# Reordering inside one attention-and-MLP kernel: batch 0's transposes, batch 1's transposes, batch 2's untangling copies and value loads

## The chip, the cores and the metric

The kernel runs on one core of one Trainium2 chip, as one launch. The metric is the device time of a run in microseconds (us). [...] TensorE (PE in the profile) multiplies matrices from SBUF into PSUM, VectorE (DVE), ScalarE (ACT) and GpSimd (POOL) work on elements, and DMAs are issued from the queues of SyncE (SP), ScalarE and GpSimd.

## The reference

Eight batches, eight heads, 576 tokens of 64 dimensions. Attention with a causal mask and a decay (from the cumulated logarithm of a forget gate f), then a two-layer MLP with exact GELU over the 4608 tokens of 512 features:

```python
scores = scale * np.matmul(q, k.transpose(0, 1, 3, 2))
log_f = np.log(np.clip(f, 0.0001, 1.0)); cum = np.cumsum(log_f, axis=-1)
decay = cum[:, :, :, None] - cum[:, :, None, :]
scores = np.where(causal, -1000000000.0, scores + decay)
attn = softmax(scores)                      # over the keys
x = np.matmul(attn, v).transpose(0, 2, 1, 3).reshape(B * S, H * D)
h = x @ w_in                                # 512 -> 2048
out = (0.5 * h * (1.0 + erf(h / sqrt(2)))) @ w_out   # 2048 -> 512
```

## The kernel before

All order is written out by hand: what an engine does next is what the Python text emits next for it.

Heads go in four pairs per batch. A pair needs q and k with the head dimension on partitions (tiles `qkT[0]` to `qkT[3]`, q and k side by side, each used again by the next batch). For batches 0 and 1 TensorE makes them: `transposes_first` (L217) writes q and k of a pair into two PSUM tiles by 64x64 transposes, and VectorE copies each out (L238); `transposes_both` (L240) does q and k in one run of 18 transposes into two PSUM tiles and copies twice (L257). The parameter `near` splits a copy so that the first keys are there early. From batch 2 on, a DMA transpose on SP (`transpose_dma`, L273) fills `tq` and `tk`, and `untangle(b, i)` (L278) brings one pair into token order with eight VectorE copies of 64x288 (L287).

Values are weighed by the decay: `load_v` (L129) fetches them in five pieces by key block into `v_sb`, which has one buffer, and `weigh_v` (L301) multiplies them into `vw` (L306), mostly on GpSimd. `scores` (L317) computes one of four tiles of a pair's scores, ScalarE takes the exponential (L354), and GpSimd clears the part above the diagonal (`affine_select`, L356; pair 0 of batch 1 is masked by TensorE instead). `attend` (L368) multiplies with `vw` into a PSUM tile `o`, and `normalize` (L383) divides (L388, L389) on VectorE. `x_dma` (L413) transposes the result to `xT` by a DMA on SP, from batch 2 on. Batch 0 has its own score tiles: `scores_a`, `scores_b`, `scores_c`, and `scores_t` for the last 64 queries.

PSUM has three pools of two tiles each: `s` for scores, `o` for attention, `m` for MLP sums and transposes. Two `o` buffers serve the two heads of a pair; transposes and sums borrow from the same pools.

`gemm1` (L430) is the first MLP layer with GELU on ScalarE (L450). The second layer of an earlier batch fills TensorE's time during attention: `take(fill, n)` emits n steps of it. In batch 2 that is `gemm2_third`: first `gemm2_second(0)` (L594: sums of row blocks ts 0, in `o`, and ts 1, in `m`, eight steps each, each closed by two VectorE additions, L602 and L554), then PLAN_0 (L534: ts 2 in two `o` banks, ts 3 in two `m` banks, sixteen steps each, each closed by a VectorE copy, L542, and an addition, L554), then PLAN_1 for batch 1. In batch 2 eight steps follow each of the first six score tiles, so pair 0's tiles carry gemm2_second and ts 2, pair 1's first two tiles carry ts 3, and then comes attention of pair 0. In batch 1 `gemm1_hold` keeps some layer-one products of batch 0 in SBUF (L458).

The last stage of the text, the loop over `ffb`, runs the rest of layer one of a batch and, beside it, untangles and weighs for the next batch.

Of the kernel before, what the change touches and what calls it, by code (L numbers as in the profile page):

```python
# [17 lines left out]
D = 64  # L18
# [36 lines left out]
def kernel(  # L55
# [10 lines left out]
    nc = tc.nc  # L66
# [25 lines left out]
    o_psum = ctx.enter_context(tc.tile_pool(name="o_psum", bufs=2, space=PSUM))  # L92
# [589 lines left out]
    def scores_a(i):  # L682
        scores_0([(i, 0, 0, TC)], new_e(0))

    def scores_b(i):
        scores_0([(i, 3, 3 * P, P), (i, 1, P, TC - P)], new_e(2))
# [72 lines left out]
    def first_attention():  # L759

        most = NBLK - 1

        near = (0, 16, D)

        def transposes(i, which, parts=(0, D), pool=m_psum, tag="m"):
            transposes_first(0, i, pool, tag, (which,), parts)

        warm_up(9)
        transposes_first(0, 0, o_psum, "o", (0,))
        transposes_first(0, 0, o_psum, "o", (1,), near, nc.scalar.copy)  # L770
        nc.vector.tensor_tensor_scan(
            decay[:, S - 2 :: -1],
            f_sb[:, S - 1 : 0 : -1],
            none[:, 0 : S - 1],
            2.0**80,
            Alu.mult,
            Alu.add,
        )
        warm_up(2, 2 * P)
        scores_a(0)  # L780
        scores_b(0)
        transposes(1, 0)
        transposes(1, 1, near)
        psw = o_psum.tile([P, NBLK, BH], FP32, tag="o", name="psw")
        for n in range(NBLK):
            nc.tensor.transpose(
                psw[:, n, :], decay[:, K0[n] : K0[n] + P], ident_fp[:BH, :BH]
            )
        scores_a(1)
        nc.vector.tensor_copy(wT[:, 0:4, :], psw[:, 0:4, :])  # L790
        nc.vector.tensor_copy(wT[D:P, 4, :], psw[D:P, 4, :])
        nc.vector.tensor_copy(
            vw(0)[:, :, :, D], wT[:, :, 0:H].rearrange("p n h -> p h n")
        )
        scores_b(1)
        transposes_both(0, 2, m_psum, "m")
        scores_c(0, 1)
        transposes(3, 0, pool=o_psum, tag="o")
        scores_a(2)
        transposes(3, 1, near)  # L800
        scores_b(2)
        weigh_v(0, 0, nc.vector, 0, most)
        weigh_v(0, 1, nc.vector, 0, most)
        load_w_in(0)
        load_v(0, 0, 8, nc.gpsimd, [most])
        load_w_in(1)
        weigh_v(0, 2, n1=most)
        weigh_v(0, 3, n1=most)
        load_w_in(2)
        load_qk_tokens(1, 0, 4)  # L810
        nc.gpsimd.tensor_tensor(
            vw(0)[:, :, most, 0:D],
            v_sb[:, :, most, :],
            wT[:, most, 0:H].unsqueeze(2).to_broadcast([P, H, D]),
            Alu.mult,
        )
        nc.gpsimd.memset(v_sb[:, :, 0, 0:1], 0.0)
        load_v(1, 0, 4, nc.gpsimd)
        load_w_in(3)
        load_qk_tokens(1, 4, 8)  # L820
        load_v(1, 4, 8, nc.gpsimd)
        scores_a(3)
        first_tail = scores_t(0, True)
        scores_c(2, 3)
        attend_0(0, 0)
        attend_0(0, 1)
        scores_b(3)
        attend_0(1, 0)
        attend_0(1, 1)
        first_tail()  # L830
        attend_0(2, 0)
        to_xT_0(0, nc.scalar.copy)
        second_tail = scores_t(2)
        attend_0(2, 1)
        to_xT_0(1, nc.scalar.copy)
        attend_0(3, 0)
        to_xT_0(2, nc.scalar.copy)
        second_tail()
        scores_t4()
        attend_0(3, 1)  # L840

        pss = [gemm1(0, 0, (0, 1)), gemm1(0, 1, (0, 1), spare())]
        for ffb in range(2):
            gemm1(0, ffb, (2,), pss[ffb])
        pss.append(gemm1(0, 2, (0, 1, 2), spare()))
        to_xT_0(3, nc.vector.tensor_copy)
        fourth = s_psum.tile([P, 2, 512], FP32, tag="s", name="ps1")
        pss.append(gemm1(0, 3, (0, 1, 2), fourth[:, 0, :]))
        for ffb in range(4):
            gemm1(0, ffb, (HP - 1,), pss[ffb])  # L850
# [23 lines left out]
    def attention(b):  # L874


        fill = gemm2_third() if b == 2 else gemm2_rows(b - 1, PLAN)
        counts = FILL_2 if b == 2 else FILL

        def av(i, n=0):  # L880
            for h in range(2):
                attend(b, i, h, (0, 1, 2, 3, 4))
                normalize(b, i, h)
                if h == 0:
                    take(fill, n)
            x_dma(b, i)

        for i in range(HP):
            for t in range(4):
                scores(b, i, t)  # L890
                take(fill, counts[i][t])
                if t == 1 and 0 < i < (HP if b == 2 else HP - 1):
                    av(i - 1)
                    if b == 2 and i == 1:
                        load_v(3)
                if b == 2 and (i, t) == (0, 3):
                    weigh_v(b, 2)
                    weigh_v(b, 3)
                if b > 2 and i == 0 and t == 1:
                    load_v(b + 1)  # L900
                if b > 2 and t == 0 and i < 2:
                    transpose_dma(b + 1, 4 * i, 4 * i + 4)
                if b == 2 and t == 1 and i == 1:
                    transpose_dma(3, 0, 4)
        if b == 2:
            take(fill, 4)
            av(HP - 1)
        else:
            av(HP - 2)
            take(fill, 3)  # L910
            av(HP - 1, 1)
            put_off.pop()()
        take(fill, 4)
        if b == 2:
            transpose_dma(3, 4, 8)
        take(fill, 999)

        pss = [gemm1(b, ffb, (0, 1)) for ffb in range(2)]
        for ffb in range(2):
            gemm1(b, ffb, (2,), pss[ffb])  # L920
        pss += [gemm1(b, ffb, (0, 1, 2), spare()) for ffb in (2, 3)]
        for ffb in range(4):
            gemm1(b, ffb, (3,), pss[ffb])
        more = s_psum.tile([P, 2, 512], FP32, tag="s", name="ps1")
        gemm1(b, 4, ps=more[:, 0, :])
        if b + 1 < B:
            untangle(b + 1, 0)
            weigh_v(b + 1, 0)
        x_tail(b)

    def second_attention():


        b, fill = 1, gemm2_first(0)

        def av(i, h):
            attend(b, i, h, (0, 1, 2, 3, 4))
            normalize(b, i, h)

        def transposes(i, pool, tag):  # L940
            transposes_first(b, i, pool, tag)


        nc.scalar.activation(warm[0:1, 0:1], warm[0:1, 0:1], Act.Exp)
        def tiles(i, t):
            scores(b, i, t)
            scores(b, i, t + 1)

        def run(i):
            av(i, 0)  # L950
            av(i, 1)

        tiles(0, 0)
        transposes(1, o_psum, "o")
        gemm1_hold(10)
        gemm1_hold(11)
        tiles(0, 2)
        gemm1_hold(12, nc.scalar.copy)
        transposes(2, o_psum, "o")
        tiles(1, 0)  # L960
        gemm1_hold(13)
        run(0)
        tiles(1, 2)
        gemm1_hold(14, nc.scalar.copy)
        transposes(3, o_psum, "o")
        weigh_v(1, 2)
        tiles(2, 0)
        gemm1_hold(15)
        run(1)
        weigh_v(1, 3)  # L970
        tiles(2, 2)
        take(fill, 4)
        tiles(3, 0)
        transpose_dma(2, 0, 4)
        transpose_dma(2, 4, 8)
        to_xT(b, 0, nc.vector.tensor_copy, o_psum, "o")
        to_xT(b, 1, nc.vector.tensor_copy, o_psum, "o")
        take(fill, 4)
        tiles(3, 2)
        behind(qk_of[2][1], H - 1)  # L980
        load_w_out(2)
        load_w_out(3)
        run(2)
        take(fill, 4)
        av(3, 0)
        take(fill, 4)
        both = s_psum.tile([P, 2, 1024], BF16, tag="s", name="ps_x2")
        to_xT(b, 2, nc.scalar.copy, ps=both[:, 0, 0:XC])
        av(3, 1)
        gemm1_begin(1, both)  # L990
        x_tail(1)
        load_v(2)

    for b in range(B):
# [6 lines left out]
        for ffb in range(4 if b < 2 else 5, n_ff):  # L1001
# [20 lines left out]
            elif b + 1 < B:  # L1022
                first, gap = (5, 3) if b == 1 else (1, 4)
                at, late = divmod(ffb - first, gap)
                if late == 0:
                    untangle(b + 1, at)
                if late == gap - 2 and (b > 1 or at < 2):
                    weigh_v(b + 1, at)
                if ffb == (9 if b == 1 else 14):
                    load_qk_tokens(b + 2)  # L1030
# [34 lines left out]
```

## Time and profile before

| what | us |
|---|---|
| median of 3 runs (lowest, highest) | 335.41 (334.63, 336.61) |
| the profiled execution | 335.99 |
| its span, first to last instruction | 334.2 |
| TensorE busy | 324.5 |
| ScalarE, VectorE, GpSimd busy | 206.0, 184.0, 134.2 |
| untangling copies (L287), 192 of them | 82.7 busy |
| weighing products on GpSimd (L306), 30 | 38.3 busy |
| batch 1's attention begins, batch 2's begins (first scores on TensorE) | 33.1, 67.0 |
| batch 2's first layer begins, batch 3's attention begins | 99.2, 113.8 |

Times within the execution count from the first instruction of the span. A row of the timeline names the start, the length, the engine, the source line and the operation, and merges neighbours of one kind; "x4" is four of them. In brackets stands the idle time of the engine before the row, and what ended it. In the list of waits the three numbers are the total, the number of waits and the longest one. A line of SPq or POOL with DMA in its operation is the issue of a transfer, not the transfer.

### The profile page before, as it was taken

Reading aid. Unit: us, or ns where it says so; the run is one execution under the profiler, and the core shown is the slowest. Engines: PE = TensorE matmul, PEld = TensorE weight load, DVE = VectorE, ACT = ScalarE, POOL = GpSimd, SP = SyncE. Lnnn points to the kernel's source line nnn. Section 1 sums busy time; section 2 is a strip of 40 time slices with the busy share of each in tenths; the row PEclk is TensorE's granted clock in tenths of the full one; section 3 lists DMA queues with packets and bytes.
Section 4 is the critical chain, followed back from the end, with each engine's and each line's share of the span. In section 5 each row is a group of like instructions: output and inputs, shape, how many; then the busy total and the mean of one; then the engine's idle time right before and its main releaser. Section 6 shows DMA issues by size and latency. Waiting matters only on the chain.

```text
span 334.2 us, 7948 instructions
## 1 busy us (share of the span) xinstructions
PE 324.5 (97%) x3233; PEld 169.2 (51%) x3233; DVE 184.0 (55%) x426; ACT 206.0 (62%) x298; POOL 134.2 (40%) x260
## 2 busy tenths in 40 slices
PE   8799999999999999999999999999999999999995
PEld 4554555445544466445644565455544654444443
DVE  5852755674549755894589547954796450010011
ACT  4876886964525786478736891798278846405600
POOL 8985973038327054704471354434532420000000
PEclk9999999999999999999999999999999999999998
DMA  8899999979999999489939896879600320021022
GB/s 125 193 198 220 189 185 138 180 160 160 204 179 184 152 207 156 99 131 196 190 107 140 167 204 122 125 144 186 178 2 1 103 73 31 2 88 38 2 50 77
DMA packets 94948, 44.18 MB, mean 132 GB/s; under 512 B 74176, under 2 KB 89792, under 8 KB 94912
## 3 DMA queue, kind: packets, MB, share of 16 engines
q1 hardware_dynamic: 77760, 27.16, 40.8%
q0 software_dynamic: 16752, 15.99, 30.3%
q8 instruction: 25, 0.41, 0.5%
q10 hardware_dynamic: 400, 0.52, 0.4%
q14 instruction: 11, 0.09, 0.1%
HBM read 36.85 MB, written 9.44 MB: 139 GB/s over the span
## 4 chain that ended last, share of the span: by engine, by line
PE 74%; DMA 13%; POOL 8%; DVE 3%; issue 1%; SPq 1%; POOLq 0%
PE ps L430 29%; PE ps L534 25%; PE ps L474 8%; PE o L375 7%; PE s L325 5%; DMA k<-in_k_dram 4%; DMA tq<-q 3%; DMA q<-in_k_dram 3%; DMA xT<-x 2%; POOL v_sb L169 2%; DVE qkT L287 2%; POOL v_sb L134 1%; POOL vw L306 1%; POOL q L120 1%; POOL k L120 1%
## 5 line engine op out<-in xcount | busy, mean ns | idle before, releaser
L450 ACT ACTIVATE g<-ps 128x512 bf16<-128x512 f32 x138 | 78.4, 602 | 80.7 <-PE ps L430 80.2
L430 PE MATMUL ps<-xT,w_in_sb 128*128 128x512 bf16 x512 | 114.1, 379 | 0.9 <-DMA xT<-x 0.6
L534 PE MATMUL ps<-w_out_sb,g 64*128 64x512 bf16 (+1 forms) x711 | 108.5, 377 | 0.3 <-DVE ot L554 0.3
L354 ACT ACTIVATE e<-s 128x896 bf16<-128x896 f32 x112 | 87.7, 836 | 21.5 <-PE s L325 16.4
L430 PEld LDWEIGHTS <-w_in_sb 128*128 128x128 bf16 x576 | 55.3, 98 | 68.1 <-issue 3.6
L356 POOL TENSOR_SCALAR_AFFINE_SELECT e<-e 128x256 bf16<-128x256 bf16 (+1 forms) x135 | 49.1, 384 | 88.3 <-ACT e L354 87.9
L534 PEld LDWEIGHTS <-g 64*128 64x128 bf16 (+1 forms) x711 | 40.3, 95 | 34.9 <-issue 4.8
L306 POOL TENSOR_TENSOR vw<-v_sb,wT 128x640 bf16<-128x640 f32 (+1 forms) x30 | 38.3, 1280 | 26.7 <-DMA v_sb<-in_v_dram 16.8
L287 DVE COPY qkT<-tk 64x288 bf16<-64x288 bf16 x96 | 42.0, 437 | 4.0 <-DMA tk<-k 2.4
L287 DVE COPY qkT<-tq 64x288 bf16<-64x288 bf16 x96 | 40.7, 424 | 3.6 <-DMA tq<-q 2.2
L542 DVE COPY ot<-ps 128x512 f32<-128x512 f32 x20 | 13.8, 692 | 48.1 <-PE ps L534 48.1
L325 PE MATMUL s<-qkT 64*128 64x256 bf16 (+2 forms) x336 | 37.5, 276 | 0.8 <-DVE qkT L238 0.6
L375 PEld LDWEIGHTS <-e 128*128 128x128 bf16 x840 | 30.3, 98 | 7.9 <-POOL e L356 2.5
L483 DVE COPY ot<-ps 128x512 f32<-128x512 f32 (+2 forms) x9 | 5.7, 632 | 49.6 <-PE ps L474 49.6
L375 PE MATMUL o<-vw,e 128*128 128x65 bf16 x840 | 32.3, 194 | 0.0
L389 DVE TENSOR_TENSOR x<-o,r 128x320 bf16<-128x320 f32 x56 | 27.5, 492 | 1.9
L474 PE MATMUL ps<-w_out_sb,g 128*128 128x512 bf16 (+2 forms) x144 | 28.0, 355 | 0.0
L325 PEld LDWEIGHTS <-qkT 64*128 64x128 bf16 x336 | 16.9, 94 | 19.1 <-issue 4.2
L474 PEld LDWEIGHTS <-g 128*128 128x128 bf16 x144 | 13.5, 98 | 14.5
L554 DVE TENSOR_TENSOR ot<-ot,ps 128x512 f32<-128x512 f32 x22 | 15.1, 685 | 1.1
L388 DVE RECIPROCAL r<-o 128x5 f32<-128x5 f32 x56 | 10.5, 188 | 9.1 <-PE o L375 9.1
L430 PE MATMUL ps<-tails,w_in_sb 128*128 128x512 bf16 x64 | 14.3, 377 | 0.0
(88 smaller groups left out, 181.9 us busy)
## 6 DMA issues: line engine op xcount, KB each, us to landing
out_dram<-ot SPq DMA_DIRECT2D x32, 256.0 KB, 2.3
v_sb<-in_v_dram SPq DMA_DIRECT2D x24, 256.0 KB, 5.0
q<-in_q_dram POOLq DMA_DIRECT2D x6, 576.0 KB, 6.6
k<-in_k_dram POOLq DMA_DIRECT2D x6, 576.0 KB, 8.7
v_sb<-in_v_dram POOLq DMA_DIRECT2D x17, 128.0 KB, 5.6
w_in_sb<-in_moe_w_in_dram POOLq DMA_DIRECT2D x4, 512.0 KB, 8.1
w_out_sb<-in_moe_w_out_dram POOLq DMA_DIRECT2D x4, 512.0 KB, 8.3
v_sb<-in_v_dram SPq DMA_DIRECT2D x6, 128.0 KB, 4.5
```

The lines of the kernel that those rows point to most:

```text
L287: nc.vector.tensor_copy(rows[:, odd], src[odd * D : (odd + 1) * D, 2 * i + h].rearrange("d j p -> d p j"),)
L306: eng.tensor_tensor(vw(b)[:, hs, n0:n1, 0:D], v_sb[:, hs, n0:n1, :], w.unsqueeze(3).to_broadcast([P, 2, n1 - n0, D]), Alu.mult,)
L325: nc.tensor.matmul(st[:, h, c + z : c + w], kT[i][d, K0[n] : K0[n] + P], qT[i][d, q0 + z : q0 + w], start=c == 0 or not on_pe, stop=not on_pe,
L354: nc.scalar.activation(et[:, :, z:c], st[:, :, z:c], Act.Exp, scale=scale)
L356: nc.gpsimd.affine_select(out=et[:, :, c0 + z : c0 + P], in_=et[:, :, c0 + z : c0 + P], compare_op=Alu.is_ge, fill=0.0, base=z, pattern=[[ ...
L375: nc.tensor.matmul(o[:, m, :], e_of[b, i, t][:, h, c : c + P], vw_of[b][:, 2 * i + h, n, :], start=(n == 0), stop=(n == m),)
L389: nc.vector.tensor_tensor(x_of[b, i][:, :, h, :], o[:, :, 0:D], r.unsqueeze(2).to_broadcast([P, NBLK, D]), Alu.mult,)
L430: nc.tensor.matmul(ps, w_in_sb[:, kt, ffb * P : (ffb + 1) * P], src[:, kt, 0:TC], start=(kt == 0), stop=(kt == n_dm - 1),)
L450: nc.scalar.activation(g_of[c][ffb], ps, Act.Gelu)
L474: nc.tensor.matmul(pss[ts][:, c0:c1], g_of[c][kt][:, ts * P : (ts + 1) * P], w_out_sb[:, kt, c0:c1], start=(kt == 0), stop=(kt == n_ff - 1),)
L534: nc.tensor.matmul(banks[r], g_of[c][kt][rows, ts * P : (ts + 1) * P], w_out_sb[rows, kt, :], start=kt == (steps.index("r") if r else 0), ...
L554: nc.vector.tensor_tensor(ot, ot, bank, Alu.add)
```

## The change

Batch 0: q of pair 1 is transposed between the first two score tiles. Pair 2's q and k are transposed one by one around `scores_b(1)`, with the copies of the decay weights in between, and pair 3's in one run (before: pair 2's in one run, pair 3's one by one). The first attention matmuls come ahead of the tail scores. Batch 1: pair 2's transposes come behind attention of pair 0. Batch 2: pairs 2 and 3 are untangled in the attention stage, after the steps of the second and the third score tile, not in the loop of layer one of batch 1; the values of batch 3 are loaded by GpSimd in three portions, not by SP in one.

```diff
@@ first_attention @@
-        def transposes(i, which, parts=(0, D), pool=m_psum, tag="m"):
-            transposes_first(0, i, pool, tag, (which,), parts)
+        def transposes(i, which, parts=(0, D)):
+            transposes_first(0, i, m_psum, "m", (which,), parts)
...
         scores_a(0)
+        transposes(1, 0)
         scores_b(0)
-        transposes(1, 0)
         transposes(1, 1, near)
...
         scores_a(1)
+        transposes(2, 0)
+        scores_b(1)
         nc.vector.tensor_copy(wT[:, 0:4, :], psw[:, 0:4, :])
+        transposes(2, 1, near)
         nc.vector.tensor_copy(wT[D:P, 4, :], psw[D:P, 4, :])
...
-        scores_b(1)
-        transposes_both(0, 2, m_psum, "m")
         scores_c(0, 1)
-        transposes(3, 0, pool=o_psum, tag="o")
         scores_a(2)
-        transposes(3, 1, near)
+        transposes_both(0, 3, m_psum, "m")
         scores_b(2)
...
         scores_a(3)
-        first_tail = scores_t(0, True)
         scores_c(2, 3)
         attend_0(0, 0)
+        first_tail = scores_t(0, True)
         attend_0(0, 1)
@@ attention(b) @@
                 if t == 1 and 0 < i < (HP if b == 2 else HP - 1):
                     av(i - 1)
-                    if b == 2 and i == 1:
-                        load_v(3)
+                if b == 2 and i == 0 and t in (1, 2):
+                    untangle(b, t + 1)
+                if b == 2 and i > 1 and t == 0:
+                    load_v(3, eng=nc.gpsimd, ns=(2 * i - 4, 2 * i - 3))
...
         if b == 2:
+            load_v(3, eng=nc.gpsimd, ns=(4,))
             transpose_dma(3, 4, 8)
@@ second_attention @@
         gemm1_hold(12, nc.scalar.copy)
-        transposes(2, o_psum, "o")
         tiles(1, 0)
         gemm1_hold(13)
         run(0)
+        transposes(2, o_psum, "o")
         tiles(1, 2)
@@ the loop over ffb @@
-                if late == 0:
+                if late == 0 and (b > 1 or at < 2):
                     untangle(b + 1, at)
```

## The prediction

> **What bounds the kernel now.** I read the page first, then TensorE's waits, then the order of VectorE and GpSimd around the start of batch 2, which most of the change moves.
>
> ```profile
> PE 324.5 (97%) x3233; PEld 169.2 (51%) x3233; DVE 184.0 (55%) x426; ACT 206.0 (62%) x298; POOL 134.2 (40%) x260
> ```
>
> TensorE is busy for 324.5 of 334.2 us, so an edit gains only what it takes out of the 9.7 us of gaps and loses whatever gap it opens. Its waits by name, longest in total first:
>
> ```profile
> PE ps L430 <- DMA xT<-x: 0.6, 2, 0.4
> ...
> PE ps L534 <- DVE ot L554: 0.3, 1, 0.3
> ```
>
> Both can be won here. The second comes at 71 us: PLAN_0's matmuls (L534) wait for the sum that empties their PSUM bank. The timeline of VectorE shows why the sum is late (start, length, then who):
>
> ```profile
> 68.90 1.34 DVE L287 COPY qkT<-tk 64x288 bf16<-64x288 bf16 x4
> 70.28 0.69 DVE L602 TENSOR_TENSOR ot<-ot,ps 128x512 f32<-128x512 f32 x1
> 71.00 0.69 DVE L554 TENSOR_TENSOR ot<-ot,ps 128x512 f32<-128x512 f32 x1
> 71.61 0.68 DVE L602 TENSOR_TENSOR ot<-ot,ps 128x512 f32<-128x512 f32 x1
> 72.32 0.69 DVE L554 TENSOR_TENSOR ot<-ot,ps 128x512 f32<-128x512 f32 x1
> 75.52 0.69 DVE L542 COPY ot<-ps 128x512 f32<-128x512 f32 x1 [2.52 <-PE ps L534]
> ```
>
> The first sums stand behind the last untangling copies (L287), 16 of which run from 64.83 to 70.25, 0.34 apart. GpSimd is idle until 71.99, then runs without a gap:
>
> ```profile
> 71.99 1.28 POOL L306 TENSOR_TENSOR vw<-v_sb,wT 128x640 bf16<-128x640 f32 x1 [16.77 <-DMA v_sb<-in_v_dram]
> ...
> 73.38 1.27 POOL L306 TENSOR_TENSOR vw<-v_sb,wT 128x640 bf16<-128x640 f32 x1
> ...
> 74.73 0.84 POOL L120 DMA_DIRECT2D q<-in_q_dram  x1
> 75.56 0.78 POOL L120 DMA_DIRECT2D k<-in_k_dram  x1
> 76.34 1.72 POOL L356 TENSOR_SCALAR_AFFINE_SELECT e<-e 128x256 bf16<-128x256 bf16 x5
> 78.03 1.27 POOL L306 TENSOR_TENSOR vw<-v_sb,wT 128x640 bf16<-128x640 f32 x1
> ```
>
> **Batch 0.** No instruction is added: pair 3 takes the joint transposes (18, then copies of 1.78 us) that pair 2 had, and pair 2 the two single sets. In order, with these rows: pair 1's q copy can start at 7.55 (end of the scan) instead of 7.83, so scores_a(1) goes at 8.60 (before 8.87); scores_a(2) needs only single copies and goes near 11.1 (before 12.55, its largest stall, 1.0). But scores_a(3) now needs the joint copies: the last tokens land at 11.56, transposes to 12.3, copies to 14.1, scores at 14.17 (before 14.14). ScalarE has lost 0.25 us less by then and scores_b(3) goes at 16.03 (before 16.28). The copies that weigh pair 0 and 1 follow at 14.1 as at 14.2 before. I take -0.25, between 0 (scores_a(3) alone) and -0.5 (if the tail scores, now behind the first attention matmuls, free PSUM sooner).
>
> **Batch 1.** Pair 2's transposes (0.41 us) go behind run(0). They need both buffers of the o pool, which run(0) has just filled; before, 1.3 us of scores and held gemm1 lay between run(0) and the next transposes. New order: run(0) near 38.85 (39.31, less 0.25 from batch 0, less the 0.41 of the transposes, plus 0.2 for a score buffer that ScalarE frees at 37.74), VectorE's held copy to 39.73, two reciprocals and products end at 41.05 (before 41.45), transposes end 41.5, next scores 41.5 against 40.35: +1.15 with batch 0's gain in it. Bounds: 0 (buffers free in time) to +1.4 (pair 3's transposes then wait for pair 2's copies of 1.42).
>
> **Batch 2, the untangling.** 16 copies move from 64.83 to behind the second pair of sums, and PLAN_0's bank emptying (L542 at 75.52, L554 at 76.25) stands behind all 16. Those banks are the o buffers in which attention of pair 0 accumulates, so TensorE, which started it at 79.24, waits for them. Gained: the stall at 71.03, 0.6 us from one L534 matmul to the next beyond its 0.11. The copies no longer have GpSimd idle, and that is their price:
>
> ```profile
> 102.21 1.27 DVE L287 COPY qkT<-tk 64x288 bf16<-64x288 bf16 x1
> ```
> ```profile
> 101.96 1.34 POOL L306 TENSOR_TENSOR vw<-v_sb,wT 128x640 bf16<-128x640 f32 x1
> ```
> ```profile
> 139.69 1.35 DVE L287 COPY qkT<-tk 64x288 bf16<-64x288 bf16 x1
> ```
>
> The same copy takes 1.27 instead of 0.33: begun inside a GpSimd product, it ends at 103.48, 0.18 after that product's end at 103.30. The one at 139.69 ends at 141.04, 0.16 after the DMA issue on GpSimd at 140.11 (0.77) ends. So a copy begun under a GpSimd instruction ends 0.17 after it. For the selects no row has an overlap; the nearest is GpSimd's plain copy at 54.80 (0.42), where the untangling copy also ended 0.18 after it. I let them hold; without it 0.5 us less.
>
> With batches 0 and 1 TensorE is 1.2 late: its matmuls for the second sums end at 72.2 (71.00 before), two sums of 0.72 end at 73.65, and attention would be due at 79.24 + 1.2 - 0.6 = 79.84. Copy by copy: ends 74.82 (second product), 75.17 free, 76.50 (issues), 76.95, 77.30, 77.89, 78.24 (selects), 79.48 (third product); pair 3: 80.86 (fourth product, 79.42 to 80.68), 81.36, 81.72, 82.05 (pair 1's selects), four free to 83.4. Then L542 and L554, 0.72 apart, to 84.9, the same for ts 3 to 86.3. Attention starts near 84.2, and PLAN_1's second matmul, which needs the last bank, at 86.35 against 80.60: +5.75. Batches 0 and 1 are inside that number: had TensorE come 1.2 earlier, the sum would still be near +5.5, because GpSimd's start at 71.99 is set by the landing of v. Ends: +5.0 (selects do not hold) and +6.
>
> [...]
>
> **Batch 2, v of batch 3.** SP loses this:
>
> ```profile
> 83.21 7.25 SPq L134 DMA_DIRECT2D v_sb<-in_v_dram  x5
> ```
>
> Behind it stood tokens' transposes, a store, and pair 1's xT, ready at 86.95 and issued at 94.80; pairs 2 and 3 went at 97.66, and gemm1 stalled at 100.63. Now the transposes come at 83.2 (k's waits for tokens that land at 86.21; stores and xT behind it lose nothing), and xT is in time: -0.6. GpSimd gets five issues of 0.75. Two fall at about 84.6, two at 90, where it is busy 2.45 us of 6; the fifth after the last select, so weighing pair 0 (95.17 before) waits for a landing near 99 to 101, with tails, further weighing and batch 4's tokens behind it. Attention needs it at 120.04, so the cover is some 18 us; its loss would be the difference alone. I take 0.
>
> **Clock.** By the working above TensorE would stand idle from about 79.9 (attention due at 79.84) to 84.2, then works in bursts until 86.35. Windows at the end of the kernel (length, busy times by engine, granted clock third from the right):
>
> ```profile
> 330.00:332.00 2.00, 0.11 (x2) 0.00 (x0) 0.29 (x1) 0.00 (x0) 0.00 (x0) 1.00 0.48 122
> 332.00:334.20 2.20, 0.00 (x0) 0.00 (x0) 0.00 (x0) 0.00 (x0) 0.00 (x0) 0.60 0.05 12
> ```
>
> The last matmul ends near 330.1, and a mean of 0.60 means half speed from about 332.4, 2.3 us later. At the start nine warm-up matmuls come 0.42 apart instead of 0.216: 1.9 us lost. Ends: 0 and 1.9; part of a slow stretch would fall on attention that waits anyway, so +1.5.
>
> [...]
>
> **Sum.** The profiled execution took 335.99 (span 334.2 and 1.8 around it), 0.6 above the median of 335.41. +5.75 - 0.6 + 1.5 = +6.65: 342.6 against the profiled one, 342.0 against the median.
>
> **Rivals.** *The clock holds* (or the selects don't): +5.0 or +5.75, less 0.6: 339.8 to 340.6. For it: attention's bursts; against: 2.3 us sufficed at the end. 25%.
> *Copies run free of GpSimd*: 16 at 0.34 from 73.65 end at 79.1, four bank emptyings at 81.95 against 80.60, +1.35 - 0.6: 336.2. Against it, every copy that began inside a product was stretched. 7%.
> *Not slower: GpSimd waits instead of VectorE, and batch 1's buffers are free in time.* The second sums end at 72.2, copies at 77.65, emptyings at 80.5, no later than before: -0.1 - 0.6: 334.7. It decides if a copy takes under 0.36 us beside GpSimd. 7%.
> *Half speed lasts two such stretches*: +8.5 or more, 344. 8%.
>
> **How the numbers follow.** Forecast 53%. A measurement of this kernel tells 0.5%, 1.7 us, from no change. Slower by more: forecast, holding clock and double stretch, 0.86. Same: 336.2 and half of 334.7, 0.10; the other half, should the first of these gains be larger than sized, 0.04, is faster. The range from 338.8 (+5.0 less 0.6, less 1 for other errors) to 344.0 leaves out the two free-copy cases and the tail above.
>
> **What would show it.** Right: L287 copies of 0.5 to 1.4 us between 72 and 84, L542 of ts 2 near 83.5, a TensorE wait of over 3 us on it before attention (L375) of batch 2, v_sb gone from SP, gemm1's stall at its start gone, and 1 us between run(0) and transposes in batch 1. Wrong: L287 copies all near 0.33 after 72 us, or attention of batch 2 starting before 81.

## The result and the profile after

The change makes the kernel slower: 343.84 us against 335.45, medians of six runs each (342.99 to 345.41; before 334.63 to 337.60), ratio 1.0247 with a 95% interval of 1.0206 to 1.0288. The profiled execution took 343.30 (span 341.2), before 335.99 (334.2). The prediction, 342.0 in a range of 338.8 to 344.0, had the sign and the main mechanism; it was 1.8 too low, and three of the six executions took more than 344.0. Two executions of the experiments below are left out of their ratios as slow ones: the profiled one of b3 (420.06 us at a mean clock of 0.755) and one of a1 (341.69, 0.985).

The page's line of engines and, below it, TensorE's waits (total, count, longest), both of after:

```profile
PE 322.2 (94%) x3191; PEld 169.9 (50%) x3233; DVE 189.0 (55%) x426; ACT 206.4 (60%) x298; POOL 139.1 (41%) x265
```
```profile
PE o L375 <- DVE ot L542: 4.9, 1, 4.9
PE s L637 <- DVE qkT L257: 1.4, 1, 1.4
...
PE ps L430 <- DMA xT<-x: 0.4, 1, 0.4
```

The first wait is new: attention's matmuls (L375) wait for the copy that empties their PSUM bank (L542). The second is in batch 0 (see b2), the third in the first layer of batch 5 (212.34). VectorE is 5 us busier with the same 426 instructions, so some of them take longer. Both are in the timelines of after, TensorE first (start, length, who; in brackets the wait):

```profile
78.08 1.46 PE L534 MATMUL ps<-w_out_sb,g 64*128 64x512 bf16 x12
79.69 0.38 PE L534 MATMUL ps<-w_out_sb,g 128*128 128x512 bf16 x1 [0.16 <-issue]
84.93 1.81 PE L375 MATMUL o<-vw,e 128*128 128x65 bf16 x30 [4.86 <-DVE ot L542]
```

VectorE in the same stretch:

```profile
73.14 0.69 DVE L554 TENSOR_TENSOR ot<-ot,ps 128x512 f32<-128x512 f32 x1
73.75 2.18 DVE L287 COPY qkT<-tq 64x288 bf16<-64x288 bf16 x4
75.94 5.52 DVE L287 COPY qkT<-tk 64x288 bf16<-64x288 bf16 x4
81.48 1.33 DVE L287 COPY qkT<-tq 64x288 bf16<-64x288 bf16 x4
82.82 1.33 DVE L287 COPY qkT<-tk 64x288 bf16<-64x288 bf16 x4
84.19 0.69 DVE L542 COPY ot<-ps 128x512 f32<-128x512 f32 x1
...
85.52 0.69 DVE L542 COPY ot<-ps 128x512 f32<-128x512 f32 x1
86.31 0.69 DVE L554 TENSOR_TENSOR ot<-ot,ps 128x512 f32<-128x512 f32 x1
```

VectorE is never idle here. Sixteen copies stand between the second sums (L554 at 73.14) and L542, which ran at 75.52 before. Eight of them take 0.33 each; four take 5.52 together. The next timeline, GpSimd's in after, shows beside what:

```profile
72.73 1.27 POOL L306 TENSOR_TENSOR vw<-v_sb,wT 128x640 bf16<-128x640 f32 x1
...
74.17 0.84 POOL L120 DMA_DIRECT2D q<-in_q_dram  x1
75.00 0.78 POOL L120 DMA_DIRECT2D k<-in_k_dram  x1
75.78 1.82 POOL L356 TENSOR_SCALAR_AFFINE_SELECT e<-e 128x256 bf16<-128x256 bf16 x5
77.57 1.27 POOL L306 TENSOR_TENSOR vw<-v_sb,wT 128x640 bf16<-128x640 f32 x1
...
78.96 1.27 POOL L306 TENSOR_TENSOR vw<-v_sb,wT 128x640 bf16<-128x640 f32 x1
80.18 0.22 POOL L313 CAST vw<-wT 128x10 bf16<-128x10 f32 x1
80.33 1.28 POOL L356 TENSOR_SCALAR_AFFINE_SELECT e<-e 128x256 bf16<-128x256 bf16 x3
```

The products (L306) keep their 1.27, as when VectorE is idle (1.27 at 73.38 in before), and the copies pay. The clock, as windows cut at its edges (length, busy times by engine, granted clock third from the right):

```profile
80.07:82.40 2.33, 0.00 (x1) 0.00 (x0) 2.26 (x6) 0.00 (x0) 1.54 (x5) 1.00 1.30 203
82.40:84.82 2.42, 0.00 (x0) 0.00 (x0) 2.32 (x7) 0.00 (x0) 0.00 (x0) 1.00 0.12 18
84.82:88.23 3.41, 3.30 (x38) 2.21 (x39) 3.20 (x8) 0.90 (x1) 0.00 (x0) 0.50 0.31 118
```

TensorE stands still from 80.07 at full clock; when it resumes, the clock is at half for 3.41 us. Four of the six executions have a mean clock of 0.990 (spans 341.4 to 343.3), two, the profiled one among them, 0.995 (340.8, 341.2): half speed for 3.41 us of 341 lowers the mean by 0.005, so four of the six have lost as much as two such stretches; only the profiled execution shows where its stretch lay.

By stages on TensorE (start times in the span, before to after): the first layer-one run loses a wait of 0.27 us, so that its third matmul comes at 21.85 instead of 22.18 (-0.33; b6, which does not have batch 0's edit, lacks that wait too), batch 2's first scores 67.02 to 68.39 (so batch 1 costs +1.70), batch 2's attention 79.24 to 84.93, its layer one 99.18 to 106.32, batch 3's first scores 113.75 to 120.31, end 334.2 to 341.2. SP issues no load of v in this batch any more, and layer one runs without the stall that it had at 100.63 (99.18 to 113.75 is 14.57 us before; 13.99 in after).

### The profile page after: what moved, and what is told of

Its sections match the earlier page's. It is cut to its first block, busy times and chain, and to the rows that moved or that the text cites. A ratio compares the mean times of both kernels' runs of the same rounds, so it can differ in the third digit from the quotient of the medians.

```text
span 341.2 us, 7909 instructions
## 1 busy us (share of the span) xinstructions
PE 322.2 (94%) x3191; PEld 169.9 (50%) x3233; DVE 189.0 (55%) x426; ACT 206.4 (60%) x298; POOL 139.1 (41%) x265
## 4 chain that ended last, share of the span: by engine, by line
PE 88%; DVE 6%; ACT 2%; issue 2%; DMA 1%; ACTq 0%
PE ps L430 35%; PE ps L534 23%; PE ps L474 8%; PE o L375 8%; PE s L325 6%; DVE qkT L287 3%; DMA xT<-x 1%; PE ps_w L210 1%; PE ps L594 1%; PE ps_f L228 1%; PE s L637 1%; ACT e L354 1%; PE o L703 1%; PE ps L570 1%; ACT e L673 1%
## 5 line engine op out<-in xcount | busy, mean ns | idle before, releaser
L430 PE MATMUL ps<-xT,w_in_sb 128*128 128x512 bf16 x494 | 112.5, 379 | 1.6 <-DMA xT<-x 0.4
L534 PE MATMUL ps<-w_out_sb,g 64*128 64x512 bf16 (+1 forms) x692 | 105.0, 378 | 1.6 <-issue 1.3
L534 PEld LDWEIGHTS <-g 64*128 64x128 bf16 (+1 forms) x711 | 39.6, 95 | 35.1 <-issue 5.0
L306 POOL TENSOR_TENSOR vw<-v_sb,wT 128x640 bf16<-128x640 f32 (+1 forms) x30 | 38.3, 1281 | 27.6 <-DMA v_sb<-in_v_dram 19.3
L287 DVE COPY qkT<-tk 64x288 bf16<-64x288 bf16 x96 | 46.0, 480 | 1.6
L287 DVE COPY qkT<-tq 64x288 bf16<-64x288 bf16 x96 | 41.9, 437 | 1.4
L375 PE MATMUL o<-vw,e 128*128 128x65 bf16 x840 | 33.0, 195 | 5.7 <-DVE ot L542 4.9
L325 PE MATMUL s<-qkT 64*128 64x256 bf16 (+1 forms) x336 | 37.4, 277 | 0.9 <-DVE qkT L238 0.6
L542 DVE COPY ot<-ps 128x512 f32<-128x512 f32 x20 | 13.8, 692 | 43.6 <-PE ps L534 43.5
L375 PEld LDWEIGHTS <-e 128*128 128x128 bf16 x840 | 31.0, 99 | 12.9 <-issue 6.8
L554 DVE TENSOR_TENSOR ot<-ot,ps 128x512 f32<-128x512 f32 x22 | 15.1, 685 | 1.1
```

Of the source, the lines that this page charges most:

```text
L287: nc.vector.tensor_copy(rows[:, odd], src[odd * D : (odd + 1) * D, 2 * i + h].rearrange("d j p -> d p j"),)
L306: eng.tensor_tensor(vw(b)[:, hs, n0:n1, 0:D], v_sb[:, hs, n0:n1, :], w.unsqueeze(3).to_broadcast([P, 2, n1 - n0, D]), Alu.mult,)
L325: nc.tensor.matmul(st[:, h, c + z : c + w], kT[i][d, K0[n] : K0[n] + P], qT[i][d, q0 + z : q0 + w], start=c == 0 or not on_pe, stop=not on_pe,
L375: nc.tensor.matmul(o[:, m, :], e_of[b, i, t][:, h, c : c + P], vw_of[b][:, 2 * i + h, n, :], start=(n == 0), stop=(n == m),)
L430: nc.tensor.matmul(ps, w_in_sb[:, kt, ffb * P : (ffb + 1) * P], src[:, kt, 0:TC], start=(kt == 0), stop=(kt == n_dm - 1),)
L534: nc.tensor.matmul(banks[r], g_of[c][kt][rows, ts * P : (ts + 1) * P], w_out_sb[rows, kt, :], start=kt == (steps.index("r") if r else 0), ...
```

## The experiments

The theory after the result: the untangling copies, slowed by GpSimd's products and standing before the bank emptyings, make TensorE wait; the wait costs clock on top; batch 1's order costs about 1 us, which is partly hidden in that wait; batch 0 and the loads are worth little. Each kernel is compared with before on the same chip (its medians there: 335.49 for a1 to a4, 335.14 for b1 to b4, 334.99 for b5, b6, c3 and e1). A difference from after is taken between medians of different chips, so some tenths of it can be the chip.

**a1: the change without its untangling.**

```diff
-                if b == 2 and i == 0 and t in (1, 2):
-                    untangle(b, t + 1)
...
-                if late == 0 and (b > 1 or at < 2):
+                if late == 0:
                     untangle(b + 1, at)
```

> The changed kernel with pairs 2 and 3 of batch 2 untangled in batch 1's layer-one loop again. Theory (the copies stand before the bank emptying, GpSimd holds them, attention waits, the clock falls): the 4.9 us wait and the half-speed stretch go, and the rest of the change stays: batch 0 -0.3, batch 1 +1.2, loads -0.6, so 335.7 (335 to 336.5), within 0.3% of the kernel before. Rival (the values' loads on GpSimd or batch 1 carry part of the loss): above 338.

Measured 337.07, ratio 1.0060 (1.0026 to 1.0094). VectorE and TensorE of a1:

```profile
76.48 0.69 DVE L542 COPY ot<-ps 128x512 f32<-128x512 f32 x1 [2.37 <-PE ps L534]
```
```profile
80.19 1.11 PE L375 MATMUL o<-vw,e 128*128 128x65 bf16 x30
```

VectorE now waits for TensorE, not the reverse, and attention starts without a wait. This one edit costs 6.8 us (343.84 less 337.07). What is left is 1.6 above before, more than the 335 to 336.5 expected.

**a2: before with the untangling moved, and nothing else** (a1's lines the other way round).

> The kernel before with only the untangling of pairs 2 and 3 moved. Theory: GpSimd's start near 72 sets the end of the copies, so nearly the whole loss shows without the other edits: +6 to +9, 341.5 to 344.5, and a wait of attention of batch 2 of 4.5 to 6 us. Rival (the loss needs TensorE late by batch 1's edit): under +4.

Measured 343.51, ratio 1.0239 (1.0201 to 1.0277): 8.0 us. VectorE, then TensorE, of a2:

```profile
72.89 3.49 DVE L287 COPY qkT<-tq 64x288 bf16<-64x288 bf16 x4
76.40 6.04 DVE L287 COPY qkT<-tk 64x288 bf16<-64x288 bf16 x4
82.45 1.54 DVE L287 COPY qkT<-tq 64x288 bf16<-64x288 bf16 x4
84.01 1.34 DVE L287 COPY qkT<-tk 64x288 bf16<-64x288 bf16 x4
```
```profile
86.12 1.81 PE L375 MATMUL o<-vw,e 128*128 128x65 bf16 x30 [6.90 <-DVE ot L542]
```

TensorE is at its bank earlier than in after, and the copies end later: GpSimd's first product begins at 73.12, when v has landed, against 71.34. So the end of the wait is set by GpSimd, not by TensorE: in after, a2, a4 and b4 the copy that is held longest ends 9.2 to 9.3 us after that first product begins, whenever TensorE arrives. Alone this edit costs 8.0, on top of the other three 6.8: their costs do not add. Here the clock was at half for two stretches (6.83 us from 83.73).

**a3: after, with the two products of pairs 2 and 3 later.**

```diff
-                if b == 2 and (i, t) == (0, 3):
+                if b == 2 and (i, t) == (1, 2):
                     weigh_v(b, 2)
                     weigh_v(b, 3)
```

> The changed kernel with GpSimd's weighing of pairs 2 and 3 of batch 2 moved from behind pair 0's fourth score tile to behind pair 1's third, so that two of GpSimd's four products no longer stand beside the copies. Theory (a copy waits for the GpSimd instruction under way): the copy of 3.6 us at 77 becomes one of 0.3 to 0.5, VectorE is done 2.5 to 3 us earlier, TensorE's wait falls from 4.9 to near 2 us and half speed mostly goes: 338 to 340. Rival (16 copies in front are the loss, GpSimd has no part): no change, 343.8.

Measured 340.81, ratio 1.0165 (1.0109 to 1.0220): 3.0 less than after, though 0.8 above the range expected. VectorE, GpSimd and TensorE of a3:

```profile
73.99 2.87 DVE L287 COPY qkT<-tq 64x288 bf16<-64x288 bf16 x4
76.87 2.37 DVE L287 COPY qkT<-tk 64x288 bf16<-64x288 bf16 x4
```
```profile
76.70 3.12 POOL L356 TENSOR_SCALAR_AFFINE_SELECT e<-e 128x256 bf16<-128x256 bf16 x8
...
86.29 1.28 POOL L306 TENSOR_TENSOR vw<-v_sb,wT 128x640 bf16<-128x640 f32 x1
```
```profile
82.82 1.52 PE L375 MATMUL o<-vw,e 128*128 128x65 bf16 x30 [2.51 <-DVE ot L542]
```

With two products gone from beside the copies, the second four take 2.37 instead of 5.52 and the wait falls from 4.86 to 2.51. That the copies are slowed by GpSimd is thereby shown: VectorE's own list is the same. Beside the selects alone the four still take 0.59 each on average instead of 0.33 (one 1.04, three 0.43).

**a4: after, with TensorE kept busy in the wait** by 22 matmuls that nothing reads.

```diff
+                if b == 2 and (i, t) == (1, 1):
+                    both = s_psum.tile([P, 2, 512], FP32, tag="s", name="ps_w")
+                    for _ in range(22):
+                        nc.tensor.matmul(
+                            both[:, 0, :], warm[:, 0:P], warm, start=True, stop=True
+                        )
```

> The changed kernel with 22 added matmuls of 128x512 on zeros (some 4.75 us) in TensorE's wait ahead of attention of pair 0 of batch 2, into a score buffer; their result is used by nothing. Theory (the wait lets the clock fall to half for 3.4 us or more): the wait itself stays, attention's 30 matmuls take 0.9 us instead of 1.6, no half-speed stretch, -1.7 to -3.4: 340.5 to 342. Rival (attention is slow there because of what VectorE and GpSimd do): 343.8 or more.

Measured 342.56 (342.30 to 342.87), ratio 1.0209 (1.0166 to 1.0252): 1.3 less than after, 0.6 above the range expected, and the spread shrinks from 2.4 us to 0.6. TensorE of a4:

```profile
79.91 4.91 PE L895 MATMUL ps_w<-warm 128*128 128x512 bf16 x22
84.83 1.35 PE L375 MATMUL o<-vw,e 128*128 128x65 bf16 x30
...
86.95 1.02 PE L534 MATMUL ps<-w_out_sb,g 64*128 64x512 bf16 x7 [0.25 <-DVE ot L554]
```

Attention starts when it did in after, at full clock, and ends 0.6 earlier. It still takes 1.35 instead of 1.11, not the 0.9 expected, which fits its second o bank being emptied only at 85.50 (L554). Then TensorE stands before the next bank, which also was late. So the clock's price is 1.3 by the medians; in the profiled execution with its one stretch 0.58 (attention to layer one 21.39 in after, 20.81 here, 19.95 in a1). The other 0.86 to a1 is late banks, the second of ts 2 and those of ts 3.

**b1: before with batch 1's edit alone.**

```diff
-        transposes(2, o_psum, "o")
         tiles(1, 0)
         gemm1_hold(13)
         run(0)
+        transposes(2, o_psum, "o")
```

> The kernel before with only batch 1's edit (pair 2's transposes behind attention of pair 0). Theory (both o buffers are still full): TensorE waits 1.1 to 1.3 us in front of these transposes and nothing gives it back: span +1.0 to +1.3, 336.5. Rival (the wait is given back by later waits, the sums at 71 us above all): +0.6, as the stall of 0.6 there falls away for a TensorE that comes 1.2 later, 336.1 or less.

Measured 336.23, ratio 1.0039 (1.0024 to 1.0055): +1.1. TensorE of b1:

```profile
39.14 1.11 PE L375 MATMUL o<-vw,e 128*128 128x65 bf16 x30
40.81 0.22 PE L228 MATMUL ps_f<-key_of,k 64*64 64x64 bf16 x2 [0.55 <-DVE r L388]
41.44 0.47 PE L228 MATMUL ps_f<-key_of,k 64*64 64x64 bf16 x34 [0.41 <-DVE x L389]
41.84 0.50 PE L325 MATMUL s<-qkT 64*128 64x448 bf16 x4
```

The transposes need the two o tiles that attention has just filled, and wait for both divisions. The next scores start at 41.84; before they started at 40.35, with attention only 0.17 later (39.31), so the place costs 1.66 us in the traces. By the medians it is 1.1; whether other executions of before lose 0.6 us somewhere that b1 does not is open.

**b4: after with batch 1's edit taken back.**

> The changed kernel with batch 1's edit undone. Theory (the end of the copies in batch 2 hangs on GpSimd's start, set by the landing of v, not on TensorE): TensorE comes 1.2 us earlier and waits as much longer, total -0.6 to +0.5 against the changed kernel, 343.2 to 344.3, the wait before attention 5.5 to 7 us. Rival (the costs add): -1.2, 342.6, the wait still 4.9.

Measured 343.50, ratio 1.0253 (1.0231 to 1.0275): 8.4 us above before on its chip, just as after is on its own, not 1.2 less. In its profiled execution TensorE came to batch 2 no earlier (68.63) and waited 5.15, less than the 5.5 to 7 expected, because its clock was at half from 15.01 to 18.42 in batch 0; without such a fall the comparison would be cleaner. The hiding is seen better in a1 and a2.

**b2: before with batch 0's edit alone.**

> The kernel before with only batch 0's edit. Theory: TensorE starts the first layer 0.3 us earlier, span -0.3, 335.1. Rival (the one long wait of 1.5 us for the joint copies that replaces several shorter ones leaves TensorE so little work in one stretch that the clock falls in some executions): median near 335.3, but some executions 3 to 6 us longer at a granted clock under 0.99.

Measured 335.30, ratio 1.0022 (0.9994 to 1.0050): no gain. TensorE of b2:

```profile
11.64 0.39 PE L637 MATMUL s<-qkT 64*128 64x512 bf16 x2 [0.25 <-ACT e L673]
14.67 0.39 PE L637 MATMUL s<-qkT 64*128 64x512 bf16 x2 [1.38 <-DVE qkT L257]
```

The stall of 0.98 that stood at 12.55 before is gone from pair 2 and is back at pair 3 as 1.38: the joint copies are late for whichever pair gets them. Runs above 338 us come in all three kernels in which this edit stands without the untangling (a1 three of ten, up to 341.69; b2 two of twelve; b5 below), in a1 and b2 with a mean clock of 0.977 to 0.988; before did not exceed 337.6, nor did b1, b6, c3 or the eleven other runs of b3. The clock can fall in batch 0 without this edit too: in c3's trace it is at half from 14.17 to 17.58, in a run of 335.08.

**b5: b2 with six matmuls that nothing reads ahead of scores_a(3)**, to see if that wait is where the clock is lost.

```diff
+        idle = o_psum.tile([P, TC], FP32, tag="o", name="ps_w")
+        for _ in range(6):
+            nc.tensor.matmul(idle, warm[:, 0:P], warm, start=True, stop=True)
         scores_a(3)
```

> The kernel before with batch 0's edit and six added matmuls of 128x512 on zeros in the 1.4 us wait ahead of scores_a(3), whose result nothing uses. Theory (the scatter of batch 0's edit, 334.3 to 338.9, comes from a clock that falls after that wait): all executions at a granted clock of 0.99 or more, highest below 336.5, median 334.8 to 335.2. Rival (the scatter has another source): the same scatter, some executions above 337.

Measured 335.98, ratio 1.0035 (1.0013 to 1.0057), with 338.71 and 338.17 among its twelve runs. The scatter stayed, so the wait is not its source, or not alone. In its profiled execution (338.71) the clock fell at 13.71, ahead of the added matmuls (15.22) and just behind another wait, of 1.41 us for k's tokens to land, and TensorE reached layer one at 26.09, some 4 us late. What makes batch 0 scatter stays open.

**b3 and b6: before with the loads of v on GpSimd, the same kernel run twice.**

```diff
-                    if b == 2 and i == 1:
-                        load_v(3)
+                if b == 2 and i > 1 and t == 0:
+                    load_v(3, eng=nc.gpsimd, ns=(2 * i - 4, 2 * i - 3))
...
+            load_v(3, eng=nc.gpsimd, ns=(4,))
             transpose_dma(3, 4, 8)
```

> The kernel before with only the values of batch 3 loaded by GpSimd. Theory: SP is free for xT, gemm1's wait at 100.6 us goes, span -0.6. What stands around the span, 1.8 us before and 2.1 in the changed kernel, comes from this edit: +0.3, so 335.1. Rival (GpSimd's issues hold up weighing or tokens for batch 3 or 4): a wait of TensorE after 104 us, 336 or more.

> The kernel before with only the values of batch 3 loaded by GpSimd, once more, for a profile of an undisturbed execution. Theory: the stretch from gemm1 of batch 2 to the first scores of batch 3 shrinks from 14.57 to 14.0 us (xT in time), what stands around the span grows from 1.8 to 2.15, and the median stays within 0.6 of the kernel before. Rival: that stretch stays at 14.5, and the edit only costs.

Measured 335.74 (335.48 without the execution of 420.06, the only one of b3 with a trace) and 335.32, ratios 1.0017 (1.0000 to 1.0034) and 1.0008 (0.9990 to 1.0026): no gain. In b6's trace layer one runs without its stall, but outside the span there are 2.2 us (334.77 less 332.6) where before has 1.8; every kernel with these loads has 2.1 to 2.2, every one without some 1.8.

**c3: before with only four copies late**, those of pair 3's k, behind attention of pair 0, where GpSimd has fewer products: a version that might win the stall at 71 us and lose nothing. (`untangle` gets a parameter for this: copy q, k or both.)

```diff
-                if late == 0:
-                    untangle(b + 1, at)
+                if late == 0:
+                    untangle(b + 1, at, (0,) if b == 1 and at == 3 else (0, 1))
...
+                if b == 2 and (i, t) == (1, 1):
+                    untangle(b, 3, (1,))
```

> The kernel before with one edit of another size: only the four copies of pair 3's k move, from the end of batch 1's layer-one loop to behind attention of pair 0 of batch 2, where VectorE has 2.5 us free. Theory (the sums at 69 us must not stand behind the last four copies, and nothing that empties a bank may stand behind copies beside GpSimd): the 0.5 to 0.6 us wait at 71 us goes and no other comes, span -0.5, 334.7. Rival (the copies of 0.34 become 0.4 to 1.4 beside GpSimd and hold up the next bank emptying): +0.3 or more.

Measured 335.09, ratio 0.9999 (0.9985 to 1.0013). The stall at 71 is not in its trace, and yet nothing is gained, against 0.5 expected. The traces side by side suggest why (TensorE, us between the named points):

| kernel | untangling moved | v on GpSimd | batch 2: scores to attention | layer one to batch 3's scores |
|---|---|---|---|---|
| before | no | no | 12.22 | 14.57 |
| b1 | no | no | 11.51 | 13.99 |
| b2 | no | no | 12.47 | 14.00 |
| b6 | no | yes | 11.52 | 14.00 |
| c3 | four copies | no | 11.52 | 14.00 |

The stall of the sums costs 0.7 in before and 0.95 in b2, whose row is

```profile
71.91 1.88 PE L534 MATMUL ps<-w_out_sb,g 64*128 64x512 bf16 x15 [0.35 <-DVE ot L554]
```

It is absent in b1 and b6, which also leave the copies where they were; b6 runs the same code as before up to there. The last sixteen copies start when `tq` has landed, 2.2 and 1.9 us ahead of batch 2's first scores in before and b2, 2.9 in b6 and 3.3 in b1. The stall on xT, 0.57, is absent in b1, b2 and c3, which leave v on SP, and in after a wait on xT turns up in batch 5 instead. So neither is there each time, and neither can be booked as a sure gain; how often executions without a trace have them no run shows.

**e1: after, with both untanglings behind pair 0's fourth tile**, so that the o banks are emptied first.

```diff
-                if b == 2 and i == 0 and t in (1, 2):
-                    untangle(b, t + 1)
+                if b == 2 and (i, t) == (0, 3):
+                    untangle(b, 2)
+                    untangle(b, 3)
```

> The changed kernel with the untangling of pairs 2 and 3 placed behind pair 0's fourth score tile, so behind the emptying of the two o banks (ts 2) but ahead of that of ts 3. Theory: attention of pair 0 starts in time, near 80, but 16 copies of 0.34 to 1.4 us beside two products and the selects end near 84.5, ts 3's banks are emptied by 86, and PLAN_1's matmuls wait instead, some 5 us: 341 to 343.5. Rival (only the o banks were in the way): 337.

Measured 345.13, ratio 1.0319 (1.0279 to 1.0359). VectorE and TensorE of e1:

```profile
82.01 2.30 DVE L287 COPY qkT<-tq 64x288 bf16<-64x288 bf16 x4
...
87.03 1.45 DVE L287 COPY qkT<-tk 64x288 bf16<-64x288 bf16 x4
88.51 0.69 DVE L542 COPY ot<-ps 128x512 f32<-128x512 f32 x1
```
```profile
84.39 1.11 PE L375 MATMUL o<-vw,e 128*128 128x65 bf16 x30
...
89.26 0.58 PE L534 MATMUL ps<-w_out_sb,g 64*128 64x512 bf16 x1 [3.46 <-DVE ot L542]
```

Attention is on time, and the wait comes one bank later. Few copies are slowed here (6.4 us for sixteen), yet sixteen in a row alone (5.42 us in before, 64.83 to 70.25) exceed the time between two emptyings (3.38 there, L542 at 75.52 and 78.90): it is the length of the block on VectorE as much as its neighbours. Its time stands above the range expected; the profiled execution had 6.83 us at half speed and came to batch 2 some 4.5 us late.

## Why the prediction was right, and where it was short

**The mechanism.** Every sign named under "what would show it" is there: stretched copies between 73.75 and 81.46, L542 at 84.19 (said: 83.5), a wait of 4.86 (over 3), batch 1's transposes behind two divisions with scores at 41.55 (said: 41.5). a1, a2 and a3 show cause and size. The rivals with free copies or a waiting GpSimd fall with the timelines of after and with a3. The rival with two half-speed stretches, given 8%, fits the mean clock of four of the six executions: put at 344, they took 343.58 to 345.41. The median stands 0.16 below the top of the range, so that the range held is in part luck.

**The order of the copies** was wrong though their end was nearly right. The prediction let one copy wait out one GpSimd instruction. The chain of waits of after (start, length) shows another pattern:

```profile
74.20 0.33 DVE qkT L287
74.53 0.60 DVE qkT L287
75.15 0.78 DVE qkT L287
75.94 1.03 DVE qkT L287
76.99 3.59 DVE qkT L287
80.59 0.43 DVE qkT L287
```

Beside the two DMA issues (74.17 to 75.78) three copies passed, in 0.33, 0.60 and 0.78, where the prediction had one free and one held through both (to 76.50); the last two ended 0.12 and 0.15 after the end of an issue. But the copy begun at 76.99 under the selects was held through both products that followed and the short casts behind them (L313, the last ends at 80.40), to 80.58. The end came at 84.16 instead of 83.4, and the delay of attention at 5.03 (84.93 against 79.90, a1's stage from 68.39) instead of 4.36: this term was 0.7 too small. The nearest row for the selects that the prediction had was another operation; here they held copies for 0.43 to 1.03 us.

Why GpSimd's products keep their 1.27 beside the copies, while one copy is held through several GpSimd instructions in turn (3.59), no run shows.

**The terms that held.** The later bank, 0.8 in the prediction (5.75 at PLAN_1's second matmul less 4.96 at attention), is 0.86 between a1 and a4. The clock, +1.5, is 1.3 by a4. Batches 0 and 1, +1.15, were +1.37; but batch 0's steps went otherwise than worked out (scores_b(3) at 16.38, not 16.03, before 16.28), and b2 has no gain. That batch 1's cost would mostly vanish in the wait is shown by a1 and a2, 1.6 and 8.0 alone and 8.4 together, and by b4.

**The steps that failed.** The 1.8 us between 342.0 and the median have three parts.

- From profile to profile the prediction said 342.6, and 343.30 was measured: 0.7 more. Up to batch 3's first scores it said +6.65, and +6.56 was measured, by two errors that cancel, which is luck: attention came 0.7 later than worked out (the copies), and the clock took 0.58 in this execution instead of 1.5. The 0.7 is what no term covered: 0.3 outside the span, and 0.4 behind batch 3's first scores (220.45 before, 220.89 after), most of it the longer wait on xT in batch 5.
- The profiled execution of after is one of the two with a single half-speed stretch and stands 0.5 below its median.
- The last 0.6 was taken off twice. The prediction credited the stall of the sums (0.6, inside the +5.75) and the stall on xT (0.6), both read from the profiled execution, and then subtracted the 0.6 by which this execution stood above its median, to which these stalls contribute. Other executions lack them with or without the edits, as the table above shows.

The upper bound of 1.9 for the clock came from the warm-up matmuls at the start, 0.42 apart. The granted clock in before's rows there is 1.00, so no run shows that this spacing is a half-speed stretch; what the stretches cost is shown by a4.

**The clock's place** was guessed from the end of the kernel, where it fell 2.3 us after the last matmul. In the middle it held for 4.75 us of standstill and fell just as work resumed, so that the whole stretch lay on work. The half-speed stretches are 3.41 us long in after (from 84.82) and 6.83 in a2 and e1. In a2, half speed begins at 83.73 and work at 86.12, which leaves only 1.0 us of work in the first 3.41 us, and a second 3.41 us at half speed follow; in e1, with work from 89.26 under a fall at 89.00, they follow all the same. In b4 the clock falls at 15.01 and at 83.28, 68.27 us or 20 times 3.41 apart. The standstill ahead of a fall was not always as long as in after: in the 3.41 us ahead of it TensorE stood still for only 2.41 in a3 (fall at 83.82, work again from 82.82) and was busy for 1.71 in b4 (fall at 15.01). What sets the moment of a fall no run shows, nor where the stretches lay in the executions without a trace.

## What to carry to other kernels

A copy block moved off a quiet stretch is priced by its neighbours on the other engine and by the first PSUM bank whose emptying stands behind it (here sixteen copies took 10.41 us, 73.75 to 84.16, instead of 5.42, and the bank's wait was 4.86): walk that queue instruction by instruction to the bank. Credit a stall only if a second execution, or the spread of the runs, shows that it is there each time; one profile has stalls of its own. And a long wait on TensorE can have a price of its own in clock, 1.3 us here for a wait of 4.9, which added matmuls that nothing reads can show.

## What the runs showed of the hardware that was not expected

- A 64x288 copy on VectorE, 0.33 alone, was held 3.59 us through selects, two GpSimd products and two short casts (3.58 or 3.59 in after, a2, a4 and b4), while beside GpSimd's DMA issues copies passed in 0.33 to 0.78.
- The half-speed stretches in the traces are one or two times 3.41 us, and the same kernel differs from execution to execution: of a3's four executions, with a wait of 2.51 in the profiled one, the mean clocks were 1.000, 0.995, 0.995 and 0.987.
- Five more loads issued by GpSimd go with 0.3 us more outside the span (1.8 to 2.1 or 2.2, in eight profiled executions against six). What takes this time is open.
